# Batch 0's q features: thirds 2 and 3 from one narrow product and spread by transfers, with low words made on ScalarE, equal thirds in the last batch and a replanned order

## The chip, the cores and the metric

The kernel runs on one core of a Trainium2 chip. A core has TensorE (PE: matrix products, with a separate stream of weight loads, PEld), VectorE (DVE), ScalarE (ACT), GpSimd (POOL) and SyncE (SP, which here issues nearly all transfers); each has its own queue of instructions and takes them in order. Data lie in SBUF (128 partitions) and PSUM (where products arrive), and come from DRAM by 16 DMA engines. The metric is the device time of one execution in microseconds; the time before is the median of three executions.

## The reference, cut to what matters

Four batches of a linear attention with a feature map of degree two, followed by a gated feed-forward with a mixing matrix over the 1088 positions:

```
batch, n_heads, seq, head_dim, r = 4, 4, 1088, 32, 8
def phi(x):
    a = einsum('rd,bhsd->bhsr', S1, x)
    b = einsum('rd,bhsd->bhsr', S2, x)
    return einsum('bhsi,bhsj->bhsij', a, b).reshape(*x.shape[:-1], r * r)
q_p, k_p = phi(q), phi(k)
kv = einsum('bhsf,bhsd->bhfd', k_p, v);  z = sum(k_p, axis=2)
x = einsum('bhsf,bhfd->bhsd', q_p, kv) / (einsum('bhsf,bhf->bhs', q_p, z)[..., None] + 1e-06)
h = gelu(x @ w_in);  u, v = h[..., :512], h[..., 512:]          # x: [4, 1088, 128]
v_n = (v - mean(v)) / sqrt(var(v) + 1e-06) * g_ln
v_s = einsum('ts,bsd->btd', w_sg, v_n) + b_sg[None, :, None]
out = x + (u * v_s) @ w_out
```

Inputs such as w_in and w_out arrive as 64-bit floats, which the kernel takes apart by integer operations.

## The kernel before

**Tiling.** 1088 positions are nine row tiles of 128 (the last half full); 128 channels fill the partitions. The 512 gate channels are four blocks of 128 (db 0 to 3). Positions as columns are cut into thirds, `CH` (364, 362, 362), in the last batch `CHL` (392, 392, 304); batch 0's attention uses 384 each (`CH0`). A main product is made of three passes with operands split into a high and a low part (w_h, w_l, vh, vl).

**Stages.** Batch 0's attention and the front half of its gate run alone at the start; I call this the head (class `Head`, 0 to 50.7 us). After it `Gate.main` of batch b streams the mixing products (lines 371, 373, 379), and the attention and gate front of batch b + 1 are slipped between them. At the end stands the last gate of the last batch, with its output product and transfer.

**The head.** k's features go through `pk` (line 801), `kb` and `features` (144) to the sum kv (`pkv`, 822, and `kvx`, 833 and 835). q's features are 64 products a_i * b_j per head: 128 rows for each of two halves p (two heads each) of a third c. Before, each (c, p) takes two products of 128 x 128 with 384 columns (`q2`, line 854: `sab` holds S1 or S2 with every row written out as often as it is needed, so that PE itself spreads a and b over 128 rows), a copy of a from PSUM by ACT (858) and a product by DVE (861). Then come, for each third, `q3` (`pnd`, 893), den, its reciprocal and xt (903, 906, 910; DVE), the transposition (`px`, 919), x_h (ACT, 922) and x_l (DVE, 926), and for each row tile the product with w_in's second half (`pv`, 947 to 949), gelu (ACT, 952) and statistics (DVE, 956 and 957). Row tiles are normalised in groups, `GROUPS = ((0, 2), (2, 3), (5, 4))` (first tile, number): the factors of groups 0 and 5 are worked out on DVE (315 to 338), those of group 2 are handed by DVE (709 to 711) to POOL (714 to 725). ACT normalises (343), and PE does the products of block db 0 with the matrix w_f itself (978: nine row tiles by three thirds). ACT and DVE split w_f into w_h (984) and w_l (992) meanwhile.

**64-bit words.** `split64` (677 to 700) makes floats of the pairs of 32-bit words of s, of w_in's halves (wi1, wi0) and of w_out: DVE shifts, masks and scales the high word (677 to 681), shifts the low word right by 8 (683), cuts the exponent out (684) and scales the low word by it (685).

**What sets the order.** The head is written as steps with names, engines and the steps they need (`Steps.at`). `Steps.order` is a list scheduler: it takes the step that could start first by assumed lengths, preferring the one with the longest way to the end; `HEAD` is a table of corrections to these ways. In the main stage a `Plan` places each step of the next batch at a time out of a table (`FIRST` for batch 1, `LATER` after). SP's loads stand in one queue, and a load whose data depends on an earlier step holds up what stands behind it.

**Transfers with repetition that exist already.** In batches 1 to 3 `spread` (154 to 165) writes 32 + 16 + 16 rows of a and b to DRAM (e_0d), each eight times, and reads them back in 128 partitions.

**The end.** `gate_final` (from 405) scales and gates the last piece in halves, two products follow (451), then two sums (453) and a transfer after each, on SP and on ACT.

Of the kernel before, what the change touches and what calls it, by code (L numbers as in the profile page):

```python
# [11 lines left out]
I32 = mybir.dt.int32  # L12
I64 = mybir.dt.int64
# [12 lines left out]
CHL = [(0, 392), (392, 392), (784, 304)]  # L26
CW = 392
# [8 lines left out]
WARM = 14  # L36


FIRST = [
# [6 lines left out]
]  # L46
LATER = [
# [6 lines left out]
]  # L54
HEAD = [
# [31 lines left out]
def tile_kernel(ctx: ExitStack, tc: tile.TileContext, qd, kd, vd, sd, wd, bd, wind, gd, woutd, identd, outd):  # L87
# [82 lines left out]
    class Attention:  # L170
# [47 lines left out]
        def load_q(self, ci):  # L218
            c0, cw = CH[ci]
            self.q[ci] = q = self.pool([P, 364], "qld", f"q{self.b}_{ci}")  # L220
            load(q[:, :cw], qd[self.b, :, c0 : c0 + cw])

        def q1(self, ci):
            q, cw = self.q.pop(ci), CH[ci][1]
            self.qt[ci] = qh, ql = [self.pool([P, 364], "qt", f"qt{self.b}_{ci}{i}", F32R) for i in "hl"]
            A.copy(qh[:, :cw], q[:, :cw])
            V.tensor_sub(ql[:, :cw], q[:, :cw], f32(qh[:, :cw]))
# [53 lines left out]
    class Gate:  # L281
        def __init__(self, b, pool, x):
            self.b, self.pool, self.x = b, pool, x
            self.ch = CHL if b == B - 1 else CH
# [91 lines left out]
        def spatial_l(self, z, db, ci, t):  # L376

            c0, cw = self.ch[ci]
            mm(z, lhsT=self.parts[db][0][:, t], rhs=w_l[t][:, c0 : c0 + cw], start=False, stop=(t == NT - 1))  # L379

        def unit(self, pool, db, ci):

            xh, xl = self.x
            c0, cw = self.ch[ci]
# [11 lines left out]
        def scale(self, pool, z, db, ci):  # L396
            c0, cw = self.ch[ci]
# [7 lines left out]
        def gate_final(self, pool, z, u, db, ci):  # L405

            c0, cw = self.ch[ci]
            gt = pool([P, CW], "gt", f"gt{self.b}_{db}_{ci}")[:, :cw]
            for cs in self.halves(cw):
                with tc.issue_after(self.gated) if cs.start else ExitStack():  # L410
                    V.scalar_tensor_tensor(
# [157 lines left out]
    class Steps:  # L569
# [11 lines left out]
        def order(self):  # L581
# [15 lines left out]
            for n in steps:  # L597
                far(n)
# [540 lines left out]
```

## Time and profile before

| | us |
|---|---|
| median of three executions | 360.99 |
| lowest and highest | 360.39, 363.04 |
| the profiled execution | 360.15 |
| its span, from first to last instruction | 358.0 |
| its head, to the end of line 978's products | 50.7 |
| last mixing product to last sum | 352.1 to 354.7 |

The span is measured inside the device; 2.15 us of the execution lie around it. The granted clock of TensorE was 0.998 of full speed. All times of single instructions below are of that execution and count from the start of its span. A row of a group names line, engine, operation, what it writes and reads, its number, the busy time, the mean of one in ns, and the idle time ahead of it with what ended it; a row of the timeline begins with start and duration.

### The profile page before, as it was taken

What the parts mean: (1) busy time and instruction counts of PE and PEld (TensorE: products, weight loads), DVE (VectorE), ACT (ScalarE), POOL (GpSimd) and SP (SyncE); (2) the same over time, 40 slices, a digit from 0 to 9 for tenths busy, and PEclk for the clock granted to TensorE, in tenths of its full rate; (3) what the DMA queues carried; (4) which work ended last, traced back from release to release, by engine and by line L of the source; (5) the groups of instructions that cost most, each with busy time, mean ns of one, the idle gap of its engine ahead of it and who ended that gap; (6) DMA issues with size and microseconds to landing.
All of it is one profiled execution on the core that took longest, in us unless ns stands there. A gap on an engine that the chain in (4) does not pass through costs nothing.

```text
span 358.0 us, 5455 instructions
## 1 busy us (share of the span) xinstructions
PE 349.3 (98%) x2024; PEld 321.3 (90%) x2024; DVE 249.6 (70%) x606; ACT 162.8 (45%) x355; POOL 22.0 (6%) x37
## 2 busy tenths in 40 slices
PE   8998999999999999999999999999999999999995
PEld 7875669898989999999898999999998899999994
DVE  5697899966999767637859766663696948642333
ACT  5567842425553963214546682332445595231210
POOL 0003000103010000022020000020202000000000
PEclk9999999999999999999999999999999999999999
DMA  7992001973400045583000007683000000100001
GB/s 252 407 405 101 2 0 31 214 264 61 127 21 2 0 99 126 154 249 113 2 0 23 1 0 146 143 206 91 2 0 1 2 0 23 41 0 2 0 2 62
DMA packets 18265, 30.18 MB, mean 84 GB/s; under 512 B 1984, under 2 KB 15168, under 8 KB 18240
## 3 DMA queue, kind: packets, MB, share of 16 engines
q1 hardware_dynamic: 18096, 29.77, 28.4%
q8 instruction: 16, 0.26, 0.3%
q10 hardware_dynamic: 144, 0.08, 0.1%
q14 instruction: 9, 0.07, 0.1%
HBM read 20.92 MB, written 8.91 MB: 83 GB/s over the span
## 4 chain that ended last, share of the span: by engine, by line
PE 88%; DVE 5%; ACT 4%; POOL 1%; issue 1%; DVEq 0%; POOLq 0%
PE pz L371 18%; PE pz L379 18%; PE pz L373 16%; PE pkv L200 3%; PE pu L388 2%; ACT vn L343 2%; PE pz L978 2%; PE pv L295 2%; PE po L458 2%; PE pu L390 2%; PE pu L389 2%; PE po L456 2%; PE pab L854 2%; PE pv L296 2%; PE po L457 2%; PE pv L297 2%
## 5 line engine op out<-in xcount | busy, mean ns | idle before, releaser
L371 PE MATMUL pz<-w_h,vh 128*128 128x362 f32 (+3 forms) x405 | 133.7, 332 | 0.2
L379 PE MATMUL pz<-w_l,vh 128*128 128x362 f32 (+3 forms) x405 | 129.5, 329 | 0.0
L373 PE MATMUL pz<-w_h,vl 128*128 128x364 f32 (+3 forms) x360 | 118.0, 328 | 0.0
L371 PEld LDWEIGHTS pz<-w_h,vh 128*128 128x128 f32 x405 | 75.9, 188 | 1.9 <-DVE gt L400 0.7
L379 PEld LDWEIGHTS pz<-w_l,vh 128*128 128x128 f32 x405 | 75.5, 188 | 0.4
L373 PEld LDWEIGHTS pz<-w_h,vl 128*128 128x128 f32 x360 | 67.7, 188 | 1.3 <-DVE vl L361 0.4
L400 DVE SCALAR_TENSOR_TENSOR gt<-pz,g_col,b_bc 128x362 f32<-128x362 f32 (+3 forms) x47 | 27.5, 591 | 37.4 <-PE pz L379 36.9
L426 ACT CAST gh<-gt 128x362 fp32r<-128x362 f32 (+3 forms) x47 | 23.0, 496 | 57.9 <-PE po L457 47.6
L393 ACT ACTIVATE u<-pu 128x362 f32<-128x362 f32 (+3 forms) x48 | 22.6, 472 | 33.6 <-PE pu L390 27.3
L427 DVE TENSOR_TENSOR gl<-gt,gh 128x362 fp32r<-128x362 f32 (+3 forms) x47 | 24.6, 531 | 15.6 <-ACT gh L426 15.1
L343 ACT ACTIVATE vn<-vn,nm,rs 128x512 f32<-128x512 f32 x36 | 27.3, 807 | 5.8 <-DVE nm L338 3.8
L361 DVE TENSOR_TENSOR vl<-vn,vh 128x384 fp32r<-128x384 f32 (+2 forms) x60 | 23.0, 420 | 9.0 <-ACT vh L356 8.9
L423 DVE TENSOR_TENSOR gt<-gt,u 128x362 f32<-128x362 f32 (+3 forms) x47 | 25.2, 544 | 4.0 <-ACT u L393 3.6
L266 DVE RECIPROCAL den<-den 128x362 f32<-128x362 f32 (+1 forms) x9 | 21.8, 2418 | 8.7 <-ACT den L263 8.7
L356 ACT CAST vh<-vn 128x384 fp32r<-128x384 f32 (+1 forms) x63 | 23.0, 417 | 5.4 <-PE pz L379 5.4
L300 ACT ACTIVATE vn<-pv 128x512 f32<-128x512 f32 x27 | 15.9, 599 | 12.5 <-PE pv L297 12.2
L978 PE MATMUL pz<-w_f,vn 128*128 128x362 f32 (+3 forms) x54 | 18.0, 476 | 1.3 <-ACT vn L343 1.3
L303 DVE BATCH_NORM_STATS2 st<-vn 128x6 f32<-128x512 f32 x27 | 17.8, 676 | 0.6 <-ACT vn L300 0.4
L388 PE MATMUL pu<-x_h,win_h 128*128 128x362 f32 (+3 forms) x48 | 17.0, 354 | 0.2 <-ACT u L393 0.2
L978 PEld LDWEIGHTS pz<-w_f,vn 128*128 128x128 f32 (+1 forms) x54 | 9.8, 189 | 8.0 <-ACT vn L343 2.8
L458 PE MATMUL po<-gl,wout_h 128*128 128x362 f32 (+3 forms) x47 | 15.8, 336 | 0.9 <-DVE gl L427 0.9
L144 DVE TENSOR_TENSOR kp<-pk,kb 128x256 f32<-128x256 f32 x27 | 11.3, 422 | 7.1 <-ACT kb L188 4.4
(198 smaller groups left out, 525.7 us busy)
## 6 DMA issues: line engine op xcount, KB each, us to landing
w_f<-in_w SPq DMA_DIRECT2D x9, 544.0 KB, 10.3
vx<-in_v SPq DMA_DIRECT2D x8, 288.0 KB, 4.4
k<-in_k SPq DMA_DIRECT2D x3, 576.0 KB, 5.3
e_0d<-ab SPq DMA_DIRECT2D x3, 364.0 KB, 4.4
e_0d<-ab SPq DMA_DIRECT2D x6, 182.0 KB, 5.2
e_0a<-e_0d SPq DMA_DIRECT2D x3, 364.0 KB, 4.3
e_0b<-e_0d SPq DMA_DIRECT2D x3, 364.0 KB, 4.2
q<-in_q SPq DMA_DIRECT2D x6, 181.0 KB, 2.3
```

The costliest lines, as they stand in the source:

```text
L343: A.activation(self.vn[:, t], self.vn[:, t], AF.Identity, bias=self.nm[:, t : t + 1], scale=self.rs[:, t : t + 1])
L356: A.copy(vh[:, ts], vs[:, ts])
L361: self.last = V.tensor_sub(vl[:, ts], vs[:, ts], f32(vh[:, ts]))
L371: last = mm(z, lhsT=vh[:, t], rhs=w_h[:, t, cs], start=(t == 0), stop=False)
L373: last = mm(z, lhsT=vl[:, t], rhs=w_h[:, t, cs], start=False, stop=False)
L379: mm(z, lhsT=self.parts[db][0][:, t], rhs=w_l[t][:, c0 : c0 + cw], start=False, stop=(t == NT - 1))
L388: mm(pu, lhsT=win_h[:, ws], rhs=xh[:, cs], start=True, stop=False)
L400: V.scalar_tensor_tensor(gt, z, g_col[:, db : db + 1], b_bc[:, c0 : c0 + cw], op0=ALU.mult, op1=ALU.add)
L423: V.tensor_mul(gt, gt, u)
L426: A.copy(gh, gt)
L427: V.tensor_sub(gl, gt, f32(gh))
L978: return mm(zs[ci], lhsT=g.vn[r, t, :P], rhs=w_f[t][r, c0 : c0 + cw], start=(t == 0), stop=(t == NT - 1),)
```

## The change

Four parts:

1. q's features of batch 0. Third 1 stays as it was (lines 794, 798, 801 now). For thirds 2 and 3 PE makes one narrow product each, the 64 rows of a and b without repetition (`q2n`, 812), ACT copies them into `ab` (64 x 768, line 815), and transfers do the spreading. `q_ea` writes b (rows 32 to 63) to DRAM (e0d, 821) and copies each row of a eight times into eight partitions of `qp` (824, one transfer for each half p, SBUF to SBUF). `q_eb` reads b back from DRAM into `eb`, where the block of 16 rows is repeated eight times (828). DVE multiplies `qp` by `eb` in place (`q_pn`, 831, four times). The first tile of w_f stands between the two pairs of transfers; by `WAFTER` the other loads of w_f, w_in's first half and b come behind them in SP's order.
2. `split64`: ACT makes a float of the low word (624: read as an unsigned integer and scaled by 2^-52). DVE's shift goes, and the scaling is a plain product (622).
3. The last batch uses the thirds of the others. `gate_final` and the halves go: the last piece is scaled (401), gated (409), multiplied (438) and summed (440) whole, and sent in two transfers (442 on SP, 443 on ACT).
4. `Steps.order` sorts by the times that `HEAD` now holds outright, later where a step needs it. `FIRST` and `LATER` have new numbers.

```diff
+WAFTER = ["qe"]
...
-CHL = [(0, 392), (392, 392), (784, 304)]
-CW = 392
+CW = 364
...
 HEAD = [
-    -20.069, 1.412, -2.15, 0, 2.374, 0, -1.026, 0.152, 0.006, -0.099, 2.215, 0, 0, 0, -0.694, -9.16, 1.754,
+    -0.402, 0.47, 1.383, 1.561, 2.371, 2.501, 3.567, 4.025, 4.495, 4.965, 2.404, -1.308, -0.154, 3.587, 1.186,
...
         def gate(self, pool, gt, u, db, ci):
-            c0, cw = self.ch[ci]
+            c0, cw = CH[ci]
             with tc.high_priority(AHEAD):
-                V.tensor_mul(gt, gt, u)
+                made = V.tensor_mul(gt, gt, u)
+                if (db, ci) == self.final:
+                    self.gated = made.ins
+                    return self, db, ci, gt, None
...
             if (db, ci) == self.final:
+                mm(o, lhsT=self.wf, rhs=gh, start=False, stop=True)
                 ot = pool([P, CW], "gt", f"o{self.b}_{ci}")[:, :cw]
-                for i, cs in enumerate(self.halves(cw)):
-                    mm(o[:, cs], lhsT=self.wf, rhs=gh[:, cs], start=False, stop=True, skip_group_check=True)
-                for i, cs in enumerate(self.halves(cw)):
-                    V.tensor_add(ot[:, cs], o[:, cs], self.xs[ci][:, cs])
-                    (A.dma_start if i else load)(outd[self.b, :, c0 : c0 + cw][:, cs], ot[:, cs])
+                V.tensor_add(ot, o, self.xs[ci])
+                n = cw // 2
+                load(outd[self.b, :, c0 : c0 + n], ot[:, :n])
+                A.dma_start(outd[self.b, :, c0 + n : c0 + cw], ot[:, n:])
                 return
...
+            def time(n):
+                if n not in done:
+                    done[n] = max([plan[n]] + [time(a) + 1e-3 for a in self.steps[n][3]])
+                return done[n]
+
+            plan = dict(zip(self.steps, HEAD))
+            self.log = sorted(((time(n), n) for n in self.steps), key=lambda x: x[0])
...
-                lambda: V.tensor_scalar(ei(), word(0), 8, None, op0=ALU.logical_shift_right),
                 lambda: V.tensor_scalar(g(), ti(), -(1 << 23), None, op0=ALU.bitwise_and),
-                lambda: V.scalar_tensor_tensor(e(), ei(), 2.0**-44, f32(g()), op0=ALU.mult, op1=ALU.mult),
+                lambda: V.tensor_mul(e(), e(), f32(g())),
             ]
+            self.s.at((name, "e"), "A", 0.2 + n / 1000, lambda: A.activation(e(), word(0, U32), AF.Copy, scale=2.0**-52), after, late=0.08)
...
+            ab = stage([64, 2 * 3 * P], "ab0", "ab0")
+            eb = [pool([P, NT - 1, P], "vl", f"eb0_{p}").rearrange("p t c -> p (t c)")[:, : 2 * 3 * P] for p in range(2)]
...
+            def q2n(c):
+                pab[c] = bank(f"pab0n_{c}", "ps", 3)[:64, : 3 * P]
+                mm(pab[c], lhsT=sk[:, :64], rhs=q[c], start=True, stop=True)
+
+            def q_ab(c):
+                A.copy(ab[:, 3 * P * (c - 1) : 3 * P * c], pab[c])
+
+            def q_ea():
+
+                n = 2 * 3 * P
+                st["e"] = dram.tile([32, n], F32, tag="e", name="e0d", bufs=3)
+                load(st["e"], ab[32:])
+                for p in range(2):
+                    to = qp[p][:, 1:].rearrange("q c t -> q (c t)")
+                    load(to, ab[16 * p : 16 * p + 16].unsqueeze(1).broadcast_to([16, R, n]))
+
+            def q_eb():
+                for p in range(2):
+                    load(eb[p], st["e"][16 * p : 16 * p + 16].unsqueeze(0).broadcast_to([R, 16, 2 * 3 * P]))
+
+            def q_pn(c, p):
+                V.tensor_mul(qp[p][:, c], qp[p][:, c], eb[p][:, 3 * P * (c - 1) : 3 * P * c])
...
+            at("qa", "SP", 2.15, q_ea, [("qab", 1), ("qab", 2)], late=-2000)
+            self.load(("lw", 0), 1330, lambda: load_w(0), ["qa"])
+            at("qe", "SP", 1.7, q_eb, ["qa"], late=-2500)
...
+            for t in range(1, NT):
+                self.load(("lw", t), 1330, lambda t=t: load_w(t), WAFTER)
+            self.load("win0", 1260, lambda: load(raw_win[0], wind[:, :DG]), WAFTER)
...
+            self.load("b", 1330, lambda: load(b_bc, bd.partition_broadcast(P)), WAFTER)
```

How the order moves is read from the built programs, where a row is an instruction with its line, what it writes and reads, and its size. SP's queue in the first loads, before (ident is the identity for transpositions, win_raw_134 w_in's second half):

```order
L763 DMA ident<-in_ident 128x192
L764 DMA win_raw_134<-in_w_in 128x512
L753 DMA w_f_190<-in_w 128x1088
L753 DMA w_f_195<-in_w 128x1088
L753 DMA w_f_204<-in_w 128x1088
L753 DMA w_f_209<-in_w 128x1088
L753 DMA w_f_218<-in_w 128x1088
```

and after:

```order
L702 DMA win_raw_134<-in_w_in 128x512
L852 DMA g_col<-in_g 128x4
L821 DMA e0d<-ab_145 32x768
L824 DMA qp_0_141<-ab_145 128x1x768
L824 DMA qp_1_142<-ab_145 128x1x768
L691 DMA w_f_231<-in_w 128x1088
L828 DMA eb_0_146<-e0d 128x1x768
L828 DMA eb_1_147<-e0d 128x1x768
L691 DMA w_f_281<-in_w 128x1088
L691 DMA w_f_307<-in_w 128x1088
L691 DMA w_f_315<-in_w 128x1088
```

Five transfers of the spread now stand behind w_in's second half, and eight of the nine w_f tiles behind them.

DVE behind x_l of the first third, before:

```order
L926 TENSOR_TENSOR x_l<-px_0_315,x_h 128x384
L903 TENSOR_SCALAR den_1_336<-pnd_1_320 128x12
L906 RECIPROCAL den_1_336<-den_1_336 128x12
L910 TENSOR_TENSOR xt_1_339<-pnd_1_320,den_1_336 128x384
L861 TENSOR_TENSOR qp_0_141<-pab_4_1_333,a_4_329 128x384
L956 BN_STATS st_0_355<-vn_126 128x6
```

and after:

```order
L898 TENSOR_TENSOR x_l<-px_0_295,x_h 128x384
L831 TENSOR_TENSOR qp_1_142<-qp_1_142,eb_1_147 128x384
L831 TENSOR_TENSOR qp_0_141<-qp_0_141,eb_0_146 128x384
L928 BN_STATS st_1_333<-vn_126 128x6
L929 BN_AGGR mv_127<-st_1_333 128x2
L928 BN_STATS st_0_336<-vn_126 128x6
L929 BN_AGGR mv_127<-st_0_336 128x2
L875 TENSOR_SCALAR den_1_339<-pnd_1_321 128x12
L878 RECIPROCAL den_1_339<-den_1_339 128x12
L882 TENSOR_TENSOR xt_1_342<-pnd_1_321,den_1_339 128x384
```

The second third's products, which take what the transfers bring, stand ahead of the first statistics; den and xt of that third have moved behind two statistics.

ACT at the end of the head (vn the normalised rows, wi0e the low word of w_in's first half, vh the high part of block 1), before:

```order
L343 ACTIVATE vn_126<-vn_126,nm_129,rs_128 128x512
L356 CAST vh_1_479<-vn_126 128x384
L952 ACTIVATE vn_126<-pv_8_475 128x512
L952 ACTIVATE vn_126<-pv_7_484 128x512
L952 ACTIVATE vn_126<-pv_6_489 128x512
L696 CAST win_h<-wi0t 128x512
L984 CAST w_h<-w_f_228 128x1088
L984 CAST w_h<-w_f_236 128x1088
L343 ACTIVATE vn_126<-vn_126,nm_129,rs_128 128x512 x4
```

and after:

```order
L924 ACTIVATE vn_126<-pv_7_449 128x512
L344 ACTIVATE vn_126<-vn_126,nm_129,rs_128 128x512
L924 ACTIVATE vn_126<-pv_8_453 128x512
L924 ACTIVATE vn_126<-pv_6_461 128x512
L344 ACTIVATE vn_126<-vn_126,nm_129,rs_128 128x512 x2
L956 CAST w_h<-w_f_315 128x1088
L357 CAST vh_1_503<-vn_126 128x384
L344 ACTIVATE vn_126<-vn_126,nm_129,rs_128 128x512 x2
L624 ACTIVATE wi0e<-win_raw_135 128x512
L357 CAST vh_1_503<-vn_126 128x384
L344 ACTIVATE vn_126<-vn_126,nm_129,rs_128 128x512 x2
```

A normalisation of the second group now stands between the last three gelus, and the four of the last group are no longer in a row.

More of the change, by code (lines that the diff above doesn't have):

```diff
@@ L224, in q1 @@
             q, cw = self.q.pop(ci), CH[ci][1]
[L225 removed]
+            self.qt[ci] = qh, ql = [self.pool([P, CW], "qt", f"qt{self.b}_{ci}{i}", F32R) for i in "hl"]
             A.copy(qh[:, :cw], q[:, :cw])
@@ L403, in scale @@
             return gt
[L405 to L411, printed above, removed]
-                        gt[:, cs], z[:, cs], g_col[:, db : db + 1], b_bc[:, c0 : c0 + cw][:, cs], op0=ALU.mult, op1=ALU.add
-                    )
-                self.gated = V.tensor_mul(gt[:, cs], gt[:, cs], u[:, cs]).ins
-            return self, db, ci, gt, None
-        def halves(self, cw):
-            return slice(0, cw // 2), slice(cw // 2, cw)
         def gate(self, pool, gt, u, db, ci):
-            c0, cw = self.ch[ci]
+            c0, cw = CH[ci]
             with tc.high_priority(AHEAD):
-                V.tensor_mul(gt, gt, u)
+                made = V.tensor_mul(gt, gt, u)
+                if (db, ci) == self.final:
+                    self.gated = made.ins
+                    return self, db, ci, gt, None
                 gl = pool([P, CW], "gl", f"gl{self.b}_{db}_{ci}", F32R)[:, :cw]
@@ L436, in end @@
             self.xs = []
-            for c0, cw in self.ch:
+            for c0, cw in CH:
                 self.xs.append(self.pool([P, 512], "r", f"x_f{c0}")[:, :cw])
@@ L457, in out @@
             mm(o, lhsT=wout_l[:, db], rhs=gh, start=False, stop=False)
-            mm(o, lhsT=wout_h[:, db], rhs=gl, start=False, stop=(db == NB - 1 or self.final == (db + 1, ci)))
+            mm(o, lhsT=wout_h[:, db], rhs=gl, start=False, stop=(db == NB - 1))
             if db == NB - 1:
@@ L474, in main @@
                 us = [self.unit(pool, 1, 0)]
-                zs = [bank(f"pz{self.b}_1_{c}", *(("psn", 2), ("psn", 2), ("ps", 3))[c])[:, : self.ch[c][1]] for c in range(len(self.ch))]
+                zs = [bank(f"pz{self.b}_1_{c}", *(("psn", 2), ("psn", 2), ("ps", 3))[c])[:, : CH[c][1]] for c in range(len(CH))]
                 for i in range(2 * NT):
@@ L479, in main @@
                         run(self.split(2, 3 * SPL.index(i), 3))
-                    for ci in range(len(self.ch)):
+                    for ci in range(len(CH)):
                         (self.spatial_l if i >= NT else self.spatial_h)(zs[ci], 1, ci, t)
@@ L485, in main @@
                             tick()
-                for ci in range(len(self.ch)):
+                for ci in range(len(CH)):
                     gt = self.scale(pool, zs[ci], 1, ci)
@@ L491, in main @@
             for db in range(first, NB):
-                for ci in range(len(self.ch)):
-                    cw = self.ch[ci][1]
+                for ci in range(len(CH)):
+                    cw = CH[ci][1]
                     u = self.unit(pool, db, ci)
@@ L508, in main @@
                             tick()
-                    if (db, ci) == self.final:
-                        pend.append(self.gate_final(pool, z, u, db, ci))
-                    else:
-                        pend.append(self.gate(pool, self.scale(pool, z, db, ci), u, db, ci))
+                    pend.append(self.gate(pool, self.scale(pool, z, db, ci), u, db, ci))
                     tick()
@@ L581, in order @@
         def order(self):
-            steps, way = self.steps, {}
-            users = {n: [] for n in steps}
-            for n, s in steps.items():
-                for a in s[3]:
-                    users[a].append(n)
-            def far(n):
-                if n not in way:
-                    s = steps[n]
-                    way[n] = s[1] + max(s[6], 0.0) + max([far(u) for u in users[n]] + [s[7]])
-                return way[n]
-            for n, more in zip(steps, HEAD):
-                far(n)
-                way[n] += more
@@ L597, in order @@
-            for n in steps:
-                far(n)
-            free, end, holds, given, moved = {}, {}, {}, {}, 0.0
-            left, out, rank = set(steps), [], {n: i for i, n in enumerate(steps)}
-            def ready(n):
-                eng, _, _, after, takes, _, _, _ = steps[n]
-                if any(a not in end for a in after):
-                    return None
-                t = max([end[a] for a in after] + [free.get(eng, 0.0)])
-                for _, tag, bufs in takes:
-                    k = len(holds.setdefault(tag, [])) - bufs
-                    if k >= 0:
-                        if holds[tag][k] not in given:
-                            return None
-                        t = max(t, given[holds[tag][k]])
-                return t
@@ L615, in order @@
-            while left:
-                could = {n: t for n in left if (t := ready(n)) is not None}
-                n = min(could, key=lambda n: (round(could[n], 3), rank[n] if steps[n][0] == "SP" else -way[n], rank[n]))
-                if steps[n][0] != "SP":
-                    soon = could[n] + steps[n][1]
-                    rival = [m for m in could if steps[m][0] == steps[n][0] and could[m] < soon and way[m] > way[n] + 0.5]
-                    n = max(rival, key=lambda m: way[m]) if rival else n
-                t = could[n]
-                eng, length, f, after, takes, frees, late, _ = steps[n]
-                left.remove(n)
-                free[eng] = t + length
-                if late < 0:
-                    moved = max(moved, t + length + 0.85) - late / 1000
-                    end[n] = moved + min(0.4 + 0.12 * moved, 1.25)
-                else:
-                    end[n] = t + length + late
-                for b, tag, _ in takes:
-                    holds[tag].append(b)
-                for b in frees:
-                    given[b] = end[n]
-                out.append((t, n))
@@ L638, in order @@
-            self.log = sorted(out, key=lambda x: x[0])
+            done = {}
+            def time(n):
[4 more added lines that the diff above has]
+            self.log = sorted(((time(n), n) for n in self.steps), key=lambda x: x[0])
             return self.log
@@ L871, in build @@
-            for t in range(NT):
-                self.load(("lw", t), 1330, lambda t=t: load_w(t))
-            self.load("win0", 1260, lambda: load(raw_win[0], wind[:, :DG]))
+                       ["q0"] + [("sab", i, 2 * j + h) for h in range(2)], [(("pab", j, i), QT[j][i], N[QT[j][i]])], late=0.15)
+                at(("qa", j), "A", 0.42, lambda j=j: q_a(j), [("q2", j, 0)], [], [("pab", j, 0)], late=0.1)
+                at(("qp", 0, j), "V", 0.48, lambda j=j: q_p(j), [("qa", j), ("q2", j, 1)], (), [("pab", j, 1)], late=0.1)
@@ L878, in build @@
             raw_out = []
-            self.load("wout", 1640, load_out, [("wi1", 5)])
+            self.load("wout", 1640, load_out, [("wi1", 4), ("wi1", "e")])
             self.load("g", 130, lambda: load(g_col, gd))
-            self.load("b", 1330, lambda: load(b_bc, bd.partition_broadcast(P)))
+            self.load("b", 1330, lambda: load(b_bc, bd.partition_broadcast(P)), WAFTER)
             n = 2 * (D + 1)
```

45 lines of the change are left out of this document (23 added, 22 removed), and 53 rows, old and new, of tables (FIRST, HEAD, LATER).

## The prediction

> **What bounds the kernel now.** The page comes first (its busy times, then its chain of waits by engine), then the chain in order of time, then windows over the opening stretch, in which nearly all of the change lies, and over the main stage.
>
> ```profile
> span 358.0 us, 5455 instructions
> PE 349.3 (98%) x2024; PEld 321.3 (90%) x2024; DVE 249.6 (70%) x606; ACT 162.8 (45%) x355; POOL 22.0 (6%) x37
> PE 88%; DVE 5%; ACT 4%; POOL 1%; issue 1%; DVEq 0%; POOLq 0%
> ```
>
> TensorE is busy 98% of the span and makes 88% of the chain. By that average a product removed from it is time won. The chain at the end of the opening, batch 0's front that I call the head, says something else:
>
> ```profile
> 38.92 0.59 DVE st L956
> 43.02 7.78 PE pz L978 x24
> 50.80 0.37 PE pu L388
> ```
>
> Columns: start, duration, engine, what it wrote. DVE's last statistics (st) lead to the factors of the last group of row tiles, ACT normalises it (a row further down), and only then TensorE does the last 12 spatial products (24 records of two each, 0.648 us a product) and goes over to the main stage at 50.80. Before that the chain lies on DVE. The windows (stretch, length, busy us and instructions of the engine asked for, clock, DMA share, GB/s) for PE in the head, DVE in its second half, PE, PEld, DVE, ACT and POOL in the main stage:
>
> ```profile
> 3.20:50.73 47.53, 45.78 (x223) 1.00 0.56 215
> 20.17:42.12 21.95, 17.99 (x63) 1.00 0.42 163
> 60.00:100.00 40.00, 38.77 (x239) 36.65 (x239) 33.60 (x59) 16.65 (x40) 5.15 (x5) 1.00 0.57 151
> ```
>
> PE works 45.78 of 47.53 us in the head, but DVE has 17.99 us of work in 21.95 and stands on the chain's last steps. So both nearly bound the head, and what ends last there are DVE's factors, ACT's normalisation and twelve products. The main stage is PE's alone.
>
> **The change part by part: the features of q.** Today 12 products of 384 columns make them, six copies on ACT and six products on DVE. Afterwards third 1 keeps four, two copies and two products; thirds 2 and 3 have one product each. PE loses 6 × 0.65 = 3.9 us, ACT two copies (0.96), DVE no product, though four now read SBUF alone. In exchange DVE waits for data that has gone through DRAM. DVE's order puts two of the four products directly behind x_l of third 1, ahead of nine pairs of statistics and of xt of third 2; what stands behind them waits with them. So the sum needs the moment A at which the last spread load has landed.
>
> ```profile
> 4.41 2.56 PE L801 MATMUL pk<-sk,k 128*128 128x128 f32 x18 [0.24 <-PE warm L140]
> L858 ACT COPY a<-pab 128x384 f32<-128x384 f32 x6 | 2.9, 480 | 0.4 <-PE pab L854 0.4
> 11.61 0.43 DVE L677 TENSOR_SCALAR wi1t<-win_raw 128x512 int32<-128x512 int32 x1 [1.78 <-DMA win_raw<-in_w_in]
> 14.71 0.35 DVE L833 TENSOR_TENSOR kvx<-pkv,ident 128x64 f32<-128x64 f32 x2
> 10.00:15.00 5.00, 5.00 (x34) 4.10 (x33) 2.92 (x8) 1.68 (x3) 0.00 (x0) 1.00 1.03 418
> 60.83 0.68 SPq L154 DMA_DIRECT2D e_0d<-ab  x1
> 61.56 2.01 SPq L159 DMA_DIRECT2D e_0d<-ab  x2
> e_0d<-ab SPq DMA_DIRECT2D x1, 364.0 KB, 4.0
> e_0d<-ab SPq DMA_DIRECT2D x1, 182.0 KB, 4.9
> DMA packets 48, 0.07 MB, mean 87 GB/s; under 512 B 0, under 2 KB 48, under 8 KB 48
> DMA packets 128, 0.19 MB, mean 186 GB/s; under 512 B 0, under 2 KB 128, under 8 KB 128
> ```
>
> First two rows: the k products end at 6.97; one product of third 1 and the two narrow ones, in PE's order among them (0.65 each: as many columns stream), end at 8.9 and the copy (0.48) at about 9.5. By then the queue is still carrying w_in, which DVE waits for until 11.61: the transfers before the new ones end there, so e0d does not start earlier. ACT's new order also puts the low word of w_in ahead of third 1's two copies, and it waits for that same landing: they end at 11.6 + 0.6 + 0.96 = 13.2 and DVE's two products at 14.3, still ahead of kvx (14.71), which their users need too: 0. Row five: loads that fill all 128 partitions run at 418 GB/s. The other six are the spread of a later batch, the nearest thing that this trace has to the new transfers. The first transfer reads 32 partitions, the next two 16 each; the last two rows are the bytes moved from 64.6 to 65.4 us, when only 16 partitions are read (87 GB/s), and from 62.4 to 63.4, with 32 (186 GB/s). The number of source partitions sets the rate there.
>
> - e0d, 96 KB from 32 partitions: 98,304 B / 186 GB/s = 0.5. It ends at 12.1.
> - The two loads into qp, 384 KB each, 16 source partitions each: the landings of the 364 KB transfer (60.83 + 4.0 = 64.83) and of the first 182 KB behind it (61.56 + 4.9 = 66.46) are 1.63 us apart, so 3.5 for twice the bytes, 7.0 for both. Bounds: 186 GB/s gives 4.2, 87 gives 9.0. I take 7.0, which rests on a landing of the same shape and not on a window: 19.1.
> - w_f's first tile, 544 KB at 418 GB/s: 1.33; it ends at 20.4.
> - The two eb loads from DRAM, 768 KB. The nearest row is b_bc, which too is read with repetition and fills 128 partitions:
>
> ```profile
> 15.55 0.36 SPq L880 DMA_DIRECT2D g_col<-in_g  x1
> 16.87 0.33 SPq L881 DMA_DIRECT2D b_bc<-in_bias  x1
> g_col<-in_g SPq DMA_DIRECT2D x1, 2.0 KB, 9.4
> b_bc<-in_bias SPq DMA_DIRECT2D x1, 544.0 KB, 9.5
> ```
>
> It lands at 16.87 + 9.5 = 26.37, 1.42 behind g_col (24.95): 392 GB/s, so 768 KB take 1.9 to 2.0. I take 1.9. At the least it is that; at the most the 186 GB/s of the slower kind, 4.2. A = 11.6 + 0.5 + 7.0 + 1.3 + 1.9 = 22.3.
>
> ```profile
> 20.17 0.55 DVE L926 TENSOR_TENSOR x_l<-px,x_h 128x384 fp32r<-128x384 f32 x1
> 20.64 0.16 DVE L903 TENSOR_SCALAR den<-pnd 128x12 f32<-128x12 f32 x1
> 21.57 0.55 DVE L861 TENSOR_TENSOR qp<-pab,a 128x384 f32<-128x384 f32 x1
> 22.22 0.69 DVE L956 BATCH_NORM_STATS2 st<-vn 128x6 f32<-128x512 f32 x1
> 29.47 0.17 DVE L711 TENSOR_SCALAR ny<-ny 128x3 int32<-128x3 int32 x1
> 29.55 0.55 DVE L861 TENSOR_TENSOR qp<-pab,a 128x384 f32<-128x384 f32 x1
> 30.02 0.69 DVE L956 BATCH_NORM_STATS2 st<-vn 128x6 f32<-128x512 f32 x1
> 33.52 1.52 ACT L343 ACTIVATE vn<-vn,nm,rs 128x512 f32<-128x512 f32 x2 [2.02 <-POOL nm L725]
> 36.58 2.00 ACT L952 ACTIVATE vn<-pv 128x512 f32<-128x512 f32 x3
> 42.15 2.93 ACT L343 ACTIVATE vn<-vn,nm,rs 128x512 f32<-128x512 f32 x4 [1.07 <-DVE nm L338]
> L696 ACT CAST win_h<-wi0t 128x512 fp32r<-128x512 f32 x1 | 0.6, 609 | 0.0
> L356 ACT CAST vh<-vn 128x384 fp32r<-128x384 f32 x6 | 2.9, 506 | 0.0
> ```
>
> What stands behind A, step by step with today's distances:
>
> - DVE up to the hand-over of the second norm group to POOL (ny). The five statistics, one x_l, the first group's norm and the hand-over take 7.42 today (22.22 to 29.64). In the new order two rounds of den, reciprocal and xt stand among them (20.64 to 21.57: 0.93 each) and four products at 0.47 (29.55 to 30.02). These read two SBUF operands instead of one in PSUM, which no row shows at this width; if that costs or saves 0.1 each, it is 0.4. 7.42 + 1.86 + 1.88 = 11.2.
> - POOL's norm, from ny's end to the normalisation on ACT (29.64 to 33.52): 3.9.
> - ACT's new order has a normalisation (0.8) ahead of the last two gelus (2.00 / 3 each, 1.3): 2.1. Today those gelus do not wait for POOL.
> - Last gelu to the last group's normalisation (38.58 to 42.15): 3.6. Its DVE part loses nothing.
> - Four normalisations with the low word of w_in (some 0.6, a copy of that width) and a cast (0.5) between them: today four in a row take 2.93, so 4.05.
> - PE's last nine products stand behind the last of the four: 9 × 0.648 = 5.8.
>
> Together 30.65: the head ends at 22.3 + 30.65 = 52.95 instead of 50.80, **+2.15**. Without the wait the same steps start when DVE has done x_l of third 1, today at 20.72, and some 0.3 sooner with a q product fewer ahead of it (an estimate: PE's work ahead of x_l stays): 20.4 + 30.65 = 51.05, +0.25. So the 3.9 us taken from PE lie beside DVE's, POOL's and ACT's steps and are worth nothing; that cover goes only if these steps shrink too. The ends: qp loads at 4.2 make A 19.5, before DVE is free (+0.25); at 9.0, +4.15.
>
> What the loads push back: in SP's order three w_f tiles, b, wout, four w_f tiles, w_in's first half and the last w_f tile stand behind eb. At 418 GB/s (tiles of 544 KB 1.33, b 1.4, wout and w_in of 512 KB 1.25) that is A + 13.2 = 35.5 for w_in, which DVE's new order reaches at about 38, and 36.8 for the last tile, which the products use from 47 on; the next batch's k comes behind them at 38 and is used in the main stage, past 53. Cover of 2 us at the least, and it moves with A: 0.
>
> **The low words.** One DVE operation less (0.4) and one ACT operation more (0.6) in each of four splits. Those of s and of w_in's second half lie ahead of A, which transfers set; w_in's first half is counted above; wout's lies in the main stage: 0. Without the wait the first two are worth at most 0.8 on DVE.
>
> **Equal thirds and the one final gate.** 392 + 392 + 304 = 364 + 362 + 362 = 1088 columns, in as many instructions, on a PE that idles 1.23 us in 40: 0 there (± 0.3). The retuned tables order the same work under that PE: 0, ± 1.2 at worst (that idle time wholly gone in one such stretch, or doubled). At the end:
>
> ```profile
> 352.12 0.38 DVE L411 SCALAR_TENSOR_TENSOR gt<-pz,g_col,b_bc 128x152 f32<-128x152 f32 x1 [1.39 <-PE pz L379]
> 354.11 0.54 DVE L453 TENSOR_TENSOR o<-po,x_f 128x152 f32<-128x152 f32 x2
> L400 DVE SCALAR_TENSOR_TENSOR gt<-pz,g_col,b_bc 128x362 f32<-128x362 f32 (+3 forms) x47 | 27.5, 591 | 37.4 <-PE pz L379 36.9
> L423 DVE TENSOR_TENSOR gt<-gt,u 128x362 f32<-128x362 f32 (+3 forms) x47 | 25.2, 544 | 4.0 <-ACT u L393 3.6
> ```
>
> From the last z (352.12) to the last sum (354.65) it takes 2.53 today, in halves that overlap. In one piece: 0.59 + 0.54 on DVE, 0.65 on PE (a product of this width), 0.55 for the sum, and 0.3 of hand-overs: 2.63, **+0.1**.
>
> Sum: 360.15 (the profiled execution; its span is 358.0) + 2.15 + 0.1 = 362.4. The median of the runs, 360.99, is 0.84 above that execution, so 363.2 stands against it: +0.6%. A difference under 1% (3.6 us) is not told from no change here.
>
> **The rivals.**
>
> R1, the spread is hidden. If the loads into qp were not held by their 16 source partitions, they would take 1.9 at 418 GB/s, A would be 17.2, before DVE is free at 20.4, and only the 0.25 and 0.1 remain: **361.3**. For it: the page moves 418 GB/s while TensorE works. Against it: the 87 and 186 GB/s rows, which differ only in the partitions read.
>
> R2, the end on the other side: the eb loads run on half of the 16 DMA engines. Their source is written as eight copies of a 16-row block with the copies outermost, so a queue that deals out the outermost dimension has eight pieces to deal. At half of 418 GB/s 768 KB take 3.8 instead of 1.9: A = 24.2, **365.1**, slower. It decides from A = 23.7 on, where the sum passes 364.6. For it: no load of this trace has so few outer pieces, b_bc has 128, so its rate says nothing against it. Against it: nothing but that no row shows it. The Trainium skill, DMA: Bandwidth & Descriptors, in its section on why a DMA increments its semaphore by 16 and not by 1, says that the number of engines is the largest up to 16 that divides the slowest non-unit dimension of both access patterns, and its Rules for kernel authors warn of "a leading zero-stride broadcast of c copies"; by that rule eight engines carry each eb load, which is this rival. No run here has shown it yet.
>
> R3, the average is right: PE's 3.9 us come off whole, since PE is busy 45.78 of 47.53: 360.99 - 3.9 + 0.1 = **357.2**. Against it: the chain ends the head on DVE and ACT, whose steps do not shrink.
>
> R4, later still: 87 GB/s for the qp loads and R2 together, A = 26.2: **367.1**.
>
> **How the numbers follow.** Forecast case 0.36, of which 0.06 above 364.6 (the qp loads near their slow end); R1 0.24; R2 0.32; R3 0.04; R4 0.04. Faster by over 1%: R3, 0.04. Within 1%: R1 and the rest of the forecast, 0.54. Slower: R2, R4 and 0.06, 0.42. The forecast's own range is 361.3 to 365.2. The range takes in R1 less the main stage's 1.2 (360.1) and R2 plus half of the qp loads' 2.0 (366.1); R3, R4 and the far edges are left out, about 0.13.
>
> **What would show it.** In the changed profile: qp's landings some 3.5 us apart (R1: 1); DVE idle for about 2 us ahead of the first product in line 831, released by a DMA; the two eb landings 1 us apart (R2: nearer 2); the last z of the head ending at 53.0 (51.1 by R1, 54.9 by R2); PE idle in the head 4 us more than before or beyond; the rest of the span as long as before. I am wrong if DVE finds eb there, if z ends before 50, or if the main stage between the head and the last z changes by more than 1.2 us.

## The result and the profile after

| | before | after |
|---|---|---|
| median of six executions, us | 361.08 | 372.89 |
| lowest and highest | 360.25, 363.04 | 370.48, 374.23 |
| ratio of the times, 95% interval | | 1.0329 (1.0309 to 1.0349) |
| profiled execution, its span | 360.15, 358.0 | 372.59, 370.8 |
| end of the head (start of the first product pu) | 50.73 | 63.49 |
| from there to the last gate | 301.39 | 301.20 |
| last gate to last sum | 2.53 | 2.68 |

The change costs 3.3%. Its own six executions differ by 1%, with the granted clock: 370.57 us at 0.979 of full speed, 374.05 at 0.961. All of the loss lies in the head: 63.49 - 50.73 = 12.76 of the 12.8 us by which the span grew. The page of the changed kernel, its busy times and its chain by engine:

```profile
span 370.8 us, 5425 instructions
PE 352.4 (95%) x2010; PEld 323.8 (87%) x2010; DVE 248.0 (67%) x599; ACT 163.6 (44%) x357; POOL 21.5 (6%) x37
PE 85%; DMA 4%; DVE 4%; ACT 3%; issue 2%; POOL 1%; SPq 1%
```

PE has fewer products (2010 records instead of 2024) and is nevertheless busy 3 us longer, and DMA stands in the chain, where there was none. Both are explained by the chain in order of time:

```profile
12.01 10.28 DMA w_f<-in_w
22.31 1.10 ACT w_h L956
23.41 0.39 ACT x_h L894
26.79 3.94 issue
30.73 2.80 PE pnd L865 x12
57.61 5.95 PE pz L950 x18
63.56 0.37 PE pu L389
```

The chain runs through the transfer of w_f's first tile (landed at 12.01 + 10.28 = 22.29) and over ACT to third 1's x; later PE stands still from 26.8 to 30.73, with nothing that its own queue shows. The twelve pnd products that follow take 2.80 us; before they took 1.45:

```profile
18.70 1.45 PE L893 MATMUL pnd<-kvx,qp 128*128 128x66 f32 x12
```

DVE's timeline has the reason for the standstill:

```profile
23.82 0.56 DVE L898 TENSOR_TENSOR x_l<-px,x_h 128x384 fp32r<-128x384 f32 x1 [3.22 <-ACT x_h L894]
29.60 1.03 DVE L831 TENSOR_TENSOR qp<-qp,eb 128x384 f32<-128x384 f32 x2 [5.22 <-DMA eb<-e0d]
```

DVE waits 3.22 us for x_h and 5.22 for eb. The moment A, which I had put at 22.3, is 29.6. The two loads into qp were not the cause. The chain has their issues:

```profile
10.65 0.69 SPq L824
11.38 0.59 SPq L824
```

and the list of transfers (KB each, us from issue to landing) what they took:

```profile
qp<-ab SPq DMA_DIRECT2D x1, 384.0 KB, 5.7
qp<-ab SPq DMA_DIRECT2D x1, 384.0 KB, 8.5
```

They landed at 16.35 and 19.88, 3.5 us apart, as forecast. Windows of PE's queue (length, busy time, granted clock, DMA share, GB/s) have the reason for the long products:

```profile
16.00:20.00 4.00, 2.32 (x19) 1.00 0.85 172
20.00:21.00 1.00, 0.28 (x3) 0.88 0.95 241
21.00:24.00 3.00, 0.16 (x1) 0.50 0.88 221
24.00:41.00 17.00, 12.48 (x40) 0.50 1.03 365
41.00:42.00 1.00, 1.00 (x9) 0.88 1.04 418
```

TensorE's clock is at half from 21 to 41 us. Before, the same stretch ran at full clock:

```profile
24.00:41.00 17.00, 15.69 (x64) 1.00 0.32 118
```

At the end of the program the one-piece gate behaves as worked out:

```profile
364.69 0.59 DVE L401 SCALAR_TENSOR_TENSOR gt<-pz,g_col,b_bc 128x362 f32<-128x362 f32 x1 [1.78 <-PE pz L380]
366.83 0.54 DVE L440 TENSOR_TENSOR o<-po,x_f 128x362 f32<-128x362 f32 x1 [0.52 <-PE po L438]
```

### The profile page after: what moved, and what is told of

It reads as the page before. It is cut to its first block, busy times and chain, and to the rows that moved or that the text cites. A ratio compares the mean times of both kernels' runs of the same rounds, so it can differ in the third digit from the quotient of the medians.

```text
span 370.8 us, 5425 instructions
## 1 busy us (share of the span) xinstructions
PE 352.4 (95%) x2010; PEld 323.8 (87%) x2010; DVE 248.0 (67%) x599; ACT 163.6 (44%) x357; POOL 21.5 (6%) x37
## 4 chain that ended last, share of the span: by engine, by line
PE 85%; DMA 4%; DVE 4%; ACT 3%; issue 2%; POOL 1%; SPq 1%
PE pz L372 18%; PE pz L380 18%; PE pz L374 16%; PE pkv L202 3%; DMA w_f<-in_w 3%; PE pu L389 2%; PE po L447 2%; PE pv L296 2%; PE po L445 2%; PE po L446 2%; PE pu L391 2%; PE pu L390 2%; PE pv L297 2%; PE pk L187 2%; PE pv L298 2%
## 5 line engine op out<-in xcount | busy, mean ns | idle before, releaser
L372 PE MATMUL pz<-w_h,vh 128*128 128x362 f32 (+1 forms) x405 | 134.0, 333 | 0.0
L380 PE MATMUL pz<-w_l,vh 128*128 128x362 f32 (+1 forms) x405 | 129.1, 328 | 0.0
L374 PE MATMUL pz<-w_h,vl 128*128 128x364 f32 (+1 forms) x360 | 118.4, 329 | 0.0
L401 DVE SCALAR_TENSOR_TENSOR gt<-pz,g_col,b_bc 128x362 f32<-128x362 f32 (+1 forms) x48 | 28.0, 589 | 50.9 <-PE pz L380 50.4
L415 ACT CAST gh<-gt 128x362 fp32r<-128x362 f32 (+1 forms) x47 | 23.0, 497 | 60.1 <-PE po L446 50.8
L394 ACT ACTIVATE u<-pu 128x362 f32<-128x362 f32 (+1 forms) x48 | 22.5, 473 | 25.4 <-PE pu L391 23.9
L409 DVE TENSOR_TENSOR gt<-gt,u 128x362 f32<-128x362 f32 (+1 forms) x48 | 25.7, 542 | 3.8 <-ACT u L394 3.4
L416 DVE TENSOR_TENSOR gl<-gt,gh 128x362 fp32r<-128x362 f32 (+1 forms) x47 | 24.5, 529 | 4.4 <-ACT gh L415 4.0
L389 PE MATMUL pu<-x_h,win_h 128*128 128x362 f32 (+1 forms) x48 | 17.0, 355 | 0.2 <-ACT u L394 0.2
L445 PE MATMUL po<-gh,wout_h 128*128 128x362 f32 (+1 forms) x47 | 15.9, 338 | 0.0
## 6 DMA issues: line engine op xcount, KB each, us to landing
w_f<-in_w SPq DMA_DIRECT2D x9, 544.0 KB, 11.6
```

The source lines that it names most:

```text
L372: last = mm(z, lhsT=vh[:, t], rhs=w_h[:, t, cs], start=(t == 0), stop=False)
L374: last = mm(z, lhsT=vl[:, t], rhs=w_h[:, t, cs], start=False, stop=False)
L389: mm(pu, lhsT=win_h[:, ws], rhs=xh[:, cs], start=True, stop=False)
L401: V.scalar_tensor_tensor(gt, z, g_col[:, db : db + 1], b_bc[:, c0 : c0 + cw], op0=ALU.mult, op1=ALU.add)
L409: made = V.tensor_mul(gt, gt, u)
L416: V.tensor_sub(gl, gt, f32(gh))
```

## The experiments

Each kernel but the last is the change with the edit shown; the last is the kernel before with parts of the change. First product is the first one of line 831 of the change (its number moves a little with the edits), A in the working. The first six experiments were executed once each. Since the change's own executions span 370.48 to 374.23, differences of some 2 us between their times say little by themselves, and the arguments go by the moments in the profiles.

| | first product | head end | span | time, us |
|---|---|---|---|---|
| the change | 29.60 | 63.49 | 370.8 | 372.89 |
| 128 different rows | 24.81 | 56.14 | 363.4 | 365.22 |
| eight by 16 different rows | 30.40 | 65.36 | 372.6 | 374.39 |
| w_f held back | 28.11 | 60.55 | 367.8 | 369.81 |
| all later loads held back | 27.30 | 59.51 | 366.5 | 368.52 |
| w_h behind x_h | 30.23 | 63.96 | 371.2 | 373.58 |
| TensorE kept at work | 30.35 | 60.80 | 369.1 | 370.94 |
| b by TensorE | 21.70 | 53.42 | 362.4 | 363.87 |
| b by TensorE, order mended | 21.39 | 52.47 | 361.2 | 363.08 |
| the other parts on the kernel before | none | 51.33 | 360.3 | 362.05 |

### What makes eb slow: 128 different rows

```diff
-                    load(eb[p], st["e"][16 * p : 16 * p + 16].unsqueeze(0).broadcast_to([R, 16, 2 * 3 * P]))
+                    load(eb[p], wd[:, p, : 2 * 3 * P])
```

> The two loads into eb read 128 different rows of w instead of eight copies of 16 rows of e0d; as many bytes, packets of the same 3072 bytes, the same place in the queue, the same partitions written. b's values are left out. Theory SHAPE (the eight outer copies put each load on eight engines, and there it also runs against the w_f tiles behind it): 768 KB take about 2 us behind w_f's first tile (landed at 22.3), so the first product of line 831 starts at about 24.5 instead of 29.6, when x_l of third 1 is done; the head ends at 55 (if the clock holds) to 58.5, the time is 364 to 367.5. Rival PLACE (whatever stands there shares the engines with the tiles behind it and lands late): product at 29.6, time 372.5 +- 1.

The first product came at 24.81 and the time was 365.22, as SHAPE said. From ACT's start on w_f's first tile (22.46) to DVE's on eb it took 2.3 us, where the change takes 7.3 (22.31 to 29.60). So the place in the queue is not what costs; the shape of the load is, or its source, which the next run separates. DVE's timeline has almost no wait for eb left:

```profile
24.81 1.03 DVE L831 TENSOR_TENSOR qp<-qp,eb 128x384 f32<-128x384 f32 x2 [0.28 <-DMA eb<-in_w]
```

### Copies or outer size: eight by 16 different rows

```diff
+                    load(eb[p], wd[16 * p : 16 * p + 16, :R, : 2 * 3 * P].rearrange("i r c -> r i c"))
```

> As the run with 128 different rows of w, but arranged in two dimensions, eight outside and 16 inside, that cannot be merged: no row is read twice, and the outer size is eight as in the change. b's values are left out. Theory SHAPE: as slow as the change, first product of line 831 at 29 to 30, time 372.5 +- 1. Rival SAME ROWS (eight readers of one DRAM row at a time are what is slow): product at about 24.5, time 364 to 367.5.

SHAPE held, with both numbers a little past the forecast: 30.40 and 374.39. No row is read twice here, the source is w as in the run before, and it is as slow as the change, so the repeated reading of the same 16 rows is harmless; the outer size of eight is what matters. Windows of 22.2 to 24.2 us in four kernels show the DMA engines at it (length, DVE's busy time, clock, DMA share, GB/s). The change:

```profile
22.20:24.20 2.00, 0.38 (x1) 0.50 0.92 255
```

Eight by 16 rows:

```profile
22.20:24.20 2.00, 0.25 (x1) 0.50 0.96 230
```

128 rows:

```profile
22.20:24.20 2.00, 0.23 (x1) 0.50 1.00 368
```

With an outer size of 128 the 16 engines are all busy and move 368 GB/s. With eight they are nearly all busy too, but move 230 to 255: the engines that carry eb and those that run ahead with the loads behind it (w_f tiles, b, w_out) hinder each other.

### The share of that hindrance: later loads held back

```diff
                 for p in range(2):
                     load(eb[p], st["e"][16 * p : 16 * p + 16].unsqueeze(0).broadcast_to([R, 16, 2 * 3 * P]))
+                st["hold"] = dram.tile([2, 16], F32, tag="hold", name="hold", bufs=1)
+                load(st["hold"], eb[1][:2, :16])
```

> Behind the two eb loads stands a transfer of 128 bytes that reads the second one's tile, so that SP issues no further w_f tile before eb has landed; all else as in the change. Theory SHAPE with SHARING: alone, eight engines with 3072 bytes in 0.121 us each move 203 GB/s, 768 KB take 3.9 us behind w_f's first tile: first product of line 831 at 25.5 to 26.5, head 3 to 4 us shorter, time 368 to 370. Rival OWN (the eight engines are slow by themselves, by the partitions that they write in step): product at 29 to 30 as before, time 372 or, as the tiles come later, up to 375.

The time, 369.81, lay in SHARING's range, the first product, 28.11, did not: the next batch's k load, 576 KB, had moved ahead of the held ones and ran beside eb. So the run did not separate what it was meant to. That the time fitted is luck: only 1.5 of the 2.9 us by which the head got shorter are the earlier product, the rest is a clock that came back at 34.8 instead of 41.2. The second try held the next batch's loads too:

```diff
+            with tc.issue_after(hold[0]) if b == 1 else ExitStack():
+                load(ks[b], kd[b])
```

(and the same for its v and q).

> As the run that held the w_f tiles back until eb had landed, but now the next batch's k, v and q loads are held too; in that run its k load had slipped in between. Nothing runs beside eb but the end of w_f's first tile. Theory SHARING: packets of eb near 0.121 us, first product of line 831 at 25.5 to 26.5, head some 2 us shorter than in that run, time 367 to 369. Rival OWN (the eight engines are slow by themselves): packets near 0.22 us as in the change, product at 28 or later, time 369.5 or more.

The first product, 27.30, lies between the two theories' numbers, and 368.52 within SHARING's. The packets decide. A transfer moves in packets, and the trace has a record of each; eb has 256 of 3072 bytes, a row each. Their median is 0.125 us here, 0.212 in the change, 0.244 with eight by 16 rows, and 0.121 both with 128 rows and for packets of this size in the kernel before. So SHARING holds, and OWN does not: alone, each of the engines is as fast as usual. The product came later than SHARING said; eb's last packet ended at 26.65 and DVE began 0.65 after it. The window of 22.2 to 24.2 shows how many engines carry eb:

```profile
22.20:24.20 2.00, 0.00 (x0) 0.50 0.52 166
```

A DMA share of 0.52 is eight engines of 16, at 166 GB/s, some 40% of the 418 of a full load and not far from half of the 368 with 128 rows. In the change too, between 22 and 25 us, some eight packets of eb are under way at any time. From ACT's start on w_f's first tile (22.79) to DVE's first product it took 4.5 us. So eb's 7.3 us are, in turn, 2.3 that a load with 128 outer rows takes there, 2.2 more for the eight engines, and 2.8 more for what runs beside them (differences between three profiles, one of each kernel). The neighbours suffer as well: packets of w_f and b, 4352 bytes each, take 0.29 us beside eb (24 to 27 us) instead of 0.168 in the kernel before. Why the two halves of the engines slow each other down is not shown by any run.

### The other wait: w_h behind x_h

```diff
             plan = dict(zip(self.steps, HEAD))
+            plan["whi", 0] = 20.126
```

> ACT's conversion of w_f's first tile (w_h, line 956), which waits for its landing at 22.3, is put behind x_h of third 1 instead of ahead of it. Theory: x_l of third 1 ends at about 21 instead of 24.4, but DVE's next product waits for eb as before; product at 29.6, time 372.5 +- 1. Rival CLOCK (the wait of TensorE from 20.3 on is what lowers its clock, and with x_h earlier the clock stays up into the next wait): PE's products between 24 and 41 shorter, head 1 to 3 us shorter, time 370 to 371.5.

x_l of third 1 ended at 21.07 instead of 24.38, and nothing came of it: first product 30.23, time 373.58. The wait for w_f's tile on ACT, which the working had missed, is real but lies ahead of a later one. The clock fell all the same (0.61 mean granted clock from 20 to 25, then 0.50).

### The clock: TensorE kept at work

```diff
                 pv[t] = bank(f"pv0_{t}")
+                for _ in range(5 if t == 1 else 0):
+                    mm(pv[t][:, : 3 * P], lhsT=sk, rhs=q[1], start=True, stop=True)
```

(likewise seven ahead of the second third's pnd and one ahead of the first transposition).

> The change with 13 products of 384 columns that nothing uses, put into TensorE's queue where it waits: one ahead of the transposition of third 1, five ahead of the first product of line 919, seven ahead of the attention product of third 2. The eb loads stay as slow as they are (first product of line 831 at 29.6 to 30.2). Theory CLOCK: with work in the gaps the granted clock stays at 1.00, PE's products between 30 and 41 take half as long as in the change, the head gets 3 to 4 us shorter, time 368.5 to 370. Rival LATE (the stretch behind eb is longer than the sum said for another reason, such as DMA): clock up, time 372.5 +- 1.

CLOCK held in the mechanism; the time, 370.94, was 0.9 above its range. Windows of PE:

```profile
20.00:25.00 5.00, 3.79 (x14) 1.00 0.90 219
25.00:30.00 5.00, 5.00 (x18) 1.00 1.02 258
30.00:35.00 5.00, 4.05 (x24) 1.00 1.04 406
```

The clock stays at 1.00. From the first product to the head's end it now takes 60.80 - 30.35 = 30.45; in the change it takes 33.89. The lowered clock costs 3.4 us. Other runs agree: ordered by the time that the clock stays at half behind the first product, 0 here, then 2.3, 6.2, 6.7, 11.3, 11.6 and 16.2 us (128 rows, all loads held, w_f held, w_h behind x_h, the change, eight by 16 rows), the stretch takes 30.45, 31.33, 32.21, 32.44, 33.73, 33.89 and 34.96. All of the difference lies in the first step of the chain, DVE's up to the hand-over to POOL (11.74 here, 15.20 in the change), in which DVE waits for TensorE's products; the steps behind it take 18.7 in all seven. The rest of the expected gain was lost to a first product 0.75 later and to a main stage 1.1 us longer; about half of the latter is a wait for win_l at its start, which DVE makes too late when the head ends sooner.

### Without any wait: b by TensorE

```diff
+            def q2b(c, p):
+                pab["b", c, p] = bank(f"pab0b_{c}_{p}", QB[c, p], N[QB[c, p]])[:, : 3 * P]
+                mm(pab["b", c, p], lhsT=sab[:, 1, p], rhs=q[c], start=True, stop=True)
...
-                V.tensor_mul(qp[p][:, c], qp[p][:, c], eb[p][:, 3 * P * (c - 1) : 3 * P * c])
+                V.tensor_mul(qp[p][:, c], qp[p][:, c], pab["b", c, p])
```

(q_eb and e0d are gone, w_h stands behind x_h, and the four new products have places in the order.)

> b of thirds 2 and 3 is spread by TensorE again (four products of 128 x 128 by 384 columns, read by DVE from PSUM), a alone goes through the two loads into qp; e0d and eb are gone, and w_h of w_f's first tile stands behind x_h. Nothing is left out. Theory: both waits go; x_l of third 1 ends at 21, qp has landed at 20 to 21, so the head ends at 21.1 + 30.65 = 51.7, 0.9 later than in the kernel before, time 361.0 + 0.9 + 0.1 = 362 (361 to 363). Rival CHAIN (the steps behind x_l are themselves slower in the new order than worked out): first product near 21, but head end past 53.5, time 364 or more. Rival GAIN (PE's two products less count): under 360.

9 of the 11.8 us come back: 363.87, a ratio of 1.0084 (1.0067 to 1.0101) to the kernel before. The first product starts at 21.70 without a wait, behind x_l as worked out:

```profile
21.22 0.56 DVE L902 TENSOR_TENSOR x_l<-px,x_h 128x384 fp32r<-128x384 f32 x1 [0.21 <-ACT x_h L898]
21.70 1.01 DVE L835 TENSOR_TENSOR qp<-qp,pab0b 128x384 f32<-128x384 f32 x2
```

The head ends at 53.42, between the 51.7 of the theory and the 53.5 of CHAIN, and the time lies between theirs too. CHAIN's mechanism is there: at full clock the first step behind the product takes 13.01 instead of the 11.2 worked out, while the steps behind it take 18.7 instead of 19.45. The main stage takes 1.1 us longer than before (win_l again, for about half). No gain from TensorE's two products less shows in this run, which has the other parts of the change in it too, and the replanned order is not better than the old one even when no transfer is waited for.

### A mended order

```diff
+            plan.update({("v3", 2): 37.424, ("wi0", "e"): 38.5601, ("vh", 1): 45.3795, ("wi0", 5): 42.2445, ("wi0", "hi"): 45.3791, ("wi0", "l1"): 45.3792, ("wi0", "l2"): 45.3793})
```

(and one of the four new products moved in the table, as described.)

> As the run in which TensorE spreads b, with the order mended at four places: the first normalisation of the second group stands behind the last two gelus, the last four normalisations stand in a row, the split of w_in's first half ends ahead of the first w_l, and one of the four b products stands behind the transposition. Theory CHAIN (the chain through DVE, POOL and ACT sets the head's end): last factors 1.5 to 2 us earlier (41.5 to 42 instead of 43.5), head end 51.5 to 52, the wait for win_l at the start of the main stage gone, time 361 to 362. Rival FULL (TensorE has no gaps left from 39.6 us on, so that earlier factors bring little): head end 52.5 to 53.2, time 362.5 to 363.5.

FULL's numbers: 52.47 and 363.08, a ratio of 1.0062 (1.0044 to 1.0080). The last factors came 1.1 us earlier and the wait for win_l went, which gained the main stage only 0.2 (302.36 against 302.53; before 301.39), so that wait was not most of what lengthened it. In the head PE has no gap left from 39.27 on:

```profile
39.27 13.27 PE L955 MATMUL pz<-w_f,vn 128*128 128x364 f32 x42 [0.17 <-ACT vn L344]
52.47 0.43 PE L389 MATMUL pu<-x_h,win_h 128*128 128x364 f32 x1
```

In the head the limits lie close together: with the transfers' waits gone and the chain shortened, PE bounds the end of it after all, together with the gaps that it had earlier.

### The other parts on the kernel before

```diff
-                lambda: V.tensor_scalar(ei(), word(0), 8, None, op0=ALU.logical_shift_right),
+            self.s.at((name, "e"), "A", 0.2 + n / 1000, lambda: A.activation(e(), word(0, U32), AF.Copy, scale=2.0**-52), after, late=0.08)
-CHL = [(0, 392), (392, 392), (784, 304)]
```

> The kernel before with the low words made on ScalarE, the equal thirds in the last batch and the final gate in one piece; q's features, the planner and all its tables stay as before. Theory (these parts cost and bring nothing): head end within 0.5 us of 50.7, last z to last sum 2.7 instead of 2.5, time 361.0 +- 1. Rival (one of them carries part of the loss, by ACT's queue in the head or by the tail): 362.5 or more.

362.05, a ratio of 1.0036 (1.0022 to 1.0050): 1.3 us, at the edge of the theory's range. By its profile the head ends 0.60 later, the main stage takes 0.7 longer, and the tail 0.15 (the span is 2.3 longer in that execution; the other 0.9 lie behind the last sum, until the last transfers have landed). A small loss, then, where I had worked out 0.1. Of the parts only the low words stand in the head; that they cost its 0.6 was not tried by itself. The two runs with b by TensorE lie some 1 to 2 us above this one; so much is left for the new order and the loads of a, which no run told apart. No version that was tried beats the kernel before.

## Why the prediction was wrong, step by step

- **That DVE's wait for eb sets the head's end**: right, the wait is in the profile by name. That the 3.9 us of PE are worth nothing was not shown by itself: no run took six products away and nothing else. It fits that the run without a wait, two products short, ended its head 2.7 later than before.
- **The chain behind A, 30.65 us**: close at full clock, 30.45 with TensorE kept at work, partly by luck. The first step took 11.74 for 11.2, the others together 18.71 for 19.45; with b by TensorE the first took 13.01 and the whole 31.72. In the change it took 33.89.
- **The two qp loads, 3.5 us each**: right, 3.5 apart. So a load from 16 source partitions is slow in this direction too (384 KB in 3.5 us, 112 GB/s), and R1 fell.
- **w_f's first tile, 1.33**: 2.4 (19.88 to 22.29), with eb's first packets already beside it.
- **"so 768 KB take 1.9 to 2.0. I take 1.9."** This is the step that failed: 7.3 us (22.29 to 29.60). Of the 7.3 us by which A came late, 5.4 are this load, 1.1 the w_f tile and 0.8 the qp loads. I took the rate from b_bc, which has 128 outer pieces, while eb has eight. The rival R2 had the mechanism and half of its size: it counted the eight engines (3.8), and not that SP sends w_f tiles, b and w_out right behind eb, which the other eight engines begin at once and which slow eb's packets from 0.125 us (the run with eb alone) to 0.212. The Trainium skill, DMA: Bandwidth & Descriptors, in its section on why a DMA increments its semaphore by 16 and not by 1, gives eight engines for this shape; the share of 0.52 with eb alone agrees, and so does the run with eight by 16 different rows. That rule, weighed with the row, deserved more than 0.32, and its price had to be taken with the neighbours in the queue.
- **x_l of third 1 at 20.4**: wrong, 24.38. In ACT's new order w_h of the first w_f tile stands ahead of x_h and waits for that tile. The trace of the change has w_h at 22.31 and x_h at 23.32; the working did not follow ACT's queue past gelu. Here it cost nothing, since A was later still.
- **The clock**: no case had it. Long waits of PE were forecast ("PE idle in the head 4 us more") without asking what the clock does in them, a term put at nothing without a reason: 3.4 us.
- **Main stage 0, tail + 0.1**: right in the change, -0.19 and +0.15. With the old tables the same parts cost the main stage 0.7, so its 0 is a sum of terms that were not told apart.
- **The range**: A + 7.3 and a chain 3.2 longer than worked out (33.89 for 30.65) are the 10.5 by which the head ended later than the forecast's 52.95. R4's 367.1 was the worst that I had put together, from terms taken one by one; a load slowed by its neighbours and a clock lowered by the wait come on top of each other.

## What to carry to other kernels

A spread by DMA is priced by its outermost size, by the partitions that it reads (16 here, 3.5 us for 384 KB), and by what the queue sends right behind it: a load that runs on half of the engines lets the next loads overtake and is slowed by them. Work taken off TensorE need not be worth anything where another engine's chain sets the end, and a wait that replaces it can cost twice, once as the wait and once as a lowered clock behind it. In a changed order each queue is to be followed past the changed steps, since one conversion that waits for a late tile holds everything behind it.

## What the runs showed of the hardware that I had not expected

The clock fell at about 20.8 us (0.88 is the mean of 20 to 21), only half a microsecond into the long gap, when PE had been busy for 58% of the four microseconds before (the window of 16 to 20 above). The Trainium skill, TensorE: Matmul & The Clock Gate, in the section on why this matters for your kernels, asks for no idle gaps over about 3 us; here the gaps before the fall were 0.52 and 1.16 us, so small gaps seem to count together, which no run separated. It came back after very different times. With 128 different rows PE worked from 24 on, and the clock was back at 27:

```profile
24.00:26.00 2.00, 2.00 (x5) 0.50 1.02 394
26.00:27.00 1.00, 1.00 (x5) 0.50 1.02 422
27.00:28.00 1.00, 1.00 (x11) 0.96 1.02 418
```

In the change PE worked from 30.73 on, with a gap of 0.57 us at 36.4, and the clock was not back before 41. The trace's records of the clock add one thing: in each run all its changes lie whole multiples of 3.41 us apart. It fell at 20.76 and rose at 41.24 in the change (six such steps), at 20.26 and 27.09 with 128 different rows (two), at 19.24 and 46.55 with eight by 16 rows (eight). In the step ahead of the fall PE was busy for 1.1 to 2.25 of the 3.41 us in the six runs in which it fell within the head. But a step with 2.20 kept the clock up in the run with TensorE kept at work, and in the change a step in which PE was busy throughout (31.00 to 34.41) did not bring it back. So what decides at each step stays open.
